# Linear attention and channel mix on one core: batch-wise groups in natural token order, v stationary in the K sums, list-scheduled issue, zero matmuls in early gaps

## The chip, the cores and the metric

The kernel runs on one core of one Trainium2 chip. The metric is the device time of one execution in microseconds (us). Each run has a state: it is called slow when it lies over 1.5% above the fastest of the same kernel. Engines: PE is TensorE (PEld its weight loads), DVE VectorE, ACT ScalarE, POOL GpSimd.

The runs were made on several chips.

## The reference

Four batches, four heads, 1088 tokens, head dimension 32, sketch rank 8; then a channel mix with width 128 and 1024 hidden channels.

```python
phi(x)  = outer(S1 x, S2 x)                      # 64 features per token and head
kv, z   = sum_s phi(k) v^T,  sum_s phi(k)        # over the 1088 tokens of a batch
x       = phi(q) kv / (phi(q) z + 1e-6)          # heads side by side: 128 channels
xk, xr  = mixes of x[s] and x[s-1] by mu_k, mu_r
out     = sigmoid(xr w_r) * (relu(xk w_k)^2 w_v)
```

No output of a batch can be formed before the K sums of that batch are complete; nothing ties one batch to another.

## The kernel before

It works on halves of two batches. A tile is 64 tokens of each, token `s*17+t`; half of k and q is transposed by DVE in 32x32 blocks, the other half by matmuls with the identity. The K sums have the features stationary:

```python
    def k_acc(half, gi, ab, kp):
        ...
        for t in range(t0, t1):
            for h in range(H):
                for b2 in range(2):
                    ...
                    nc.tensor.matmul(kv[hp:hp + 64, b2, (h // 2) * D:(h // 2) * D + D],
                                     kp[rows, t - t0, h].rearrange("p i j -> p (i j)"),
                                     tok["v%d" % half][rows, h, t, :], ...)
```

The order of issue is written by hand: first nearly all K work, with the q work of the first groups mixed in, then the channel mix of nine groups of up to 512 tokens, in which the q work of group g+3 is put between the matmuls of group g:

```python
    for n in range(nn + 3):
        g, cp = divmod(n, 4)
        if n < nn:
            mm1(g, cp)          # up-projection, then ReLU on ACT
        if cp == 0 and g + 3 < NQ:
            q1(g + 3)
        if cp == 1 and g + 2 < NQ:
            q5(g + 2)           # x = phi(q) kv, then PP on ACT and XK on DVE
        ...
        if n < nn:
            sq(g, cp)           # square on DVE
        if 2 <= n < nn + 2:
            mm2(*divmod(n - 2, 4))
```

`XK` is the mixed input of the up-projection: once it is written for a group, the group's eight matmuls, eight 512-column ReLUs and four squares can run.

## Time and profile before

The first three runs took 142.41, 143.49 and 229.2 us; the profiled execution has a span of 136.2 us.

| kernel before | us | share |
|---|---|---|
| PE busy | 98.8 | 73% |
| DVE busy | 78.3 | 57% |
| ACT busy | 69.2 | 51% |

No engine is full on average. Part 2 of the page, 40 equal slices of 3.4 us with the busy share in tenths, shows why: DVE and ACT have almost nothing to do from the fifth to the tenth slice and much to do in the second half.

```profile
PE   3250958659997789496929949549949689698970
DVE  3685030300158572285799595595396795977761
ACT  4010011101461423626886777674687767989950
```

The tile view of `wk`, the weights of the up-projection, says when the channel mix begins (durations in ns, then the first and last start in us):

```profile
L347 PE MATMUL h<-XK,wk x61: 270/379/634, 64.1 to 130.8; 128*128 128x512 bf16 x53, 128*128 128x256 bf16 x8
```

The first stands at 64.1 us, almost half way. The stretches of the view by windows give what each engine did from 12 to 36, from 36 to 60 and from 60 us on (after the length of the stretch the busy us of PE, PEld, DVE, ACT and POOL, each with its number of instructions in brackets; then the granted clock, the DMA share and GB/s):

```profile
12.00:36.00 24.00, 17.79 (x530) 15.89 (x534) 3.13 (x5) 2.90 (x7) 1.98 (x14) 0.93 0.76 181
36.00:60.00 24.00, 19.64 (x744) 16.88 (x736) 12.68 (x22) 9.82 (x25) 0.00 (x0) 1.00 0.02 4
60.00:136.00 76.00, 57.58 (x723) 39.53 (x730) 54.79 (x105) 54.27 (x82) 0.00 (x0) 0.97 0.08 31
```

In the first of them PE works 17.8 of 24 us and DVE 3.1. Much of PE's time before 60 us, 16.0 us in the first of these stretches and 10.7 in the second, is the K sums, lines L188 and L195: in all 9.6 + 6.5 + 11.3 = 27.4 us in the groups by form (busy us, mean ns; then the idle time before them):

```profile
L195 PE MATMUL kv<-ab 64*64 64x32 f32 x136 | 11.3, 243 | 0.0
L188 PE MATMUL kv<-tok_v_66,kp 64*64 64x32 f32 x272 | 9.6, 269 | 8.1 <-issue 4.5 <-DMA tok_v_66<-in_v_dram 3.6
L188 PE MATMUL kv<-tok_v_67,kp 64*64 64x32 f32 x272 | 6.5, 222 | 0.8 <-issue 0.8
```

### The profile page before, as it was taken

What the parts mean: (1) busy time and instruction counts of PE and PEld (TensorE: products, weight loads), DVE (VectorE), ACT (ScalarE), POOL (GpSimd) and SP (SyncE); (2) the same over time, 40 slices, a digit from 0 to 9 for tenths busy, and PEclk for the clock granted to TensorE, in tenths of its full rate; (3) what the DMA queues carried; (4) which work ended last, traced back from release to release, by engine and by line L of the source; (5) the groups of instructions that cost most, each with busy time, mean ns of one, the idle gap of its engine ahead of it and who ended that gap; (6) DMA issues with size and microseconds to landing.
All of it is one profiled execution on the core that took longest, in us unless ns stands there. A gap on an engine that the chain in (4) does not pass through costs nothing.

```text
span 136.2 us, 4574 instructions
## 1 busy us (share of the span) xinstructions
PE 98.8 (73%) x2054; PEld 75.1 (55%) x2065; DVE 78.3 (57%) x155; ACT 69.2 (51%) x117; POOL 8.4 (6%) x29
## 2 busy tenths in 40 slices
PE   3250958659997789496929949549949689698970
PEld 2140948458896658374626646346645466465650
DVE  3685030300158572285799595595396795977761
ACT  4010011101461423626886777674687767989950
POOL 7802004000000000000000000000000000000000
PEclk9999999986999999999999999986999999999998
DMA  3999999930000000000000002002002011021013
GB/s 103 335 275 305 301 248 224 302 58 5 5 5 0 5 5 5 7 0 5 0 2 5 0 0 82 0 0 77 0 0 82 0 40 42 0 77 76 5 77 115
DMA packets 5010, 9.79 MB, mean 72 GB/s; under 512 B 1520, under 2 KB 1904, under 8 KB 4992
## 3 DMA queue, kind: packets, MB, share of 16 engines
q1 hardware_dynamic: 3120, 6.69, 16.0%
q0 software_dynamic: 1856, 2.82, 8.9%
q8 instruction: 16, 0.26, 0.8%
q14 instruction: 2, 0.02, 0.0%
q10 hardware_dynamic: 16, 0.00, 0.0%
HBM read 7.80 MB, written 2.23 MB: 74 GB/s over the span
## 4 chain that ended last, share of the span: by engine, by line
PE 50%; DVE 18%; ACT 13%; DMA 8%; issue 8%; SPq 1%; DVEq 0%; ACTq 0%
PE kv L188 9%; DMA tok_v_66<-in_v_dram 8%; PE tp L154 8%; PE qtp L277 7%; PE o L367 7%; PE h L347 6%; DVE qp L270 5%; DVE XK L333 4%; PE abwp L250 4%; PE abp L166 4%; PE kv L195 3%; PE xps L317 2%; ACT PP_150 L332 2%; ACT PP_149 L332 2%; DVE den L262 1%
## 5 line engine op out<-in xcount | busy, mean ns | idle before, releaser
L174 DVE TENSOR_TENSOR kp<-ab 128x1024 f32<-128x1024 f32 (+1 forms) x10 | 10.6, 1064 | 23.3 <-ACT ab L170 23.1
L277 PE MATMUL qtp<-ident,qp 128*128 128x128 f32 x68 | 9.7, 284 | 13.9 <-DVE qp L270 11.8
L347 PE MATMUL h<-XK,wk 128*128 128x512 bf16 (+1 forms) x61 | 18.7, 374 | 0.5
L170 ACT COPY ab<-abp 128x256 f32<-128x256 f32 (+1 forms) x10 | 3.4, 341 | 26.6 <-PE abp L166 26.4
L277 PEld LDWEIGHTS qtp<-ident,qp 128*128 128x128 f32 x68 | 7.4, 142 | 16.9 <-ACT r L381 13.1
L188 PE MATMUL kv<-tok_v_66,kp 64*64 64x32 f32 x272 | 9.6, 269 | 8.1 <-issue 4.5
L188 PEld LDWEIGHTS kv<-tok_v_66,kp 64*64 64x64 f32 x272 | 8.9, 185 | 9.7 <-issue 9.7
L195 PE MATMUL kv<-ab 64*64 64x32 f32 x136 | 11.3, 243 | 0.0
L270 DVE TENSOR_TENSOR qp<-an,abw 128x1024 f32<-128x1024 f32 (+1 forms) x9 | 10.5, 1165 | 0.3
L317 PE MATMUL xps<-qpT,kvbd 128*64 128x256 f32 (+3 forms) x80 | 9.4, 359 | 0.0
L195 PEld LDWEIGHTS kv<-ab 64*64 64x64 f32 x136 | 8.6, 163 | 0.0
L283 ACT COPY qpT<-qtp 128x512 f32<-128x512 f32 (+1 forms) x9 | 5.1, 566 | 4.8 <-PE qtp L277 4.8
L166 PE MATMUL abp<-SW,kT_131 128*32 128x64 f32 x136 | 5.0, 314 | 3.5 <-DVE kT_131 L147 3.5
L285 DVE COPY qpT<-qtp 128x512 f32<-128x512 f32 (+1 forms) x9 | 5.9, 651 | 2.5 <-PE qtp L277 2.5
L188 PE MATMUL kv<-tok_v_67,kp 64*64 64x32 f32 x272 | 6.5, 222 | 0.8 <-issue 0.8
L333 DVE SCALAR_TENSOR_TENSOR XK<-xps,mu_k,PP_150 128x512 bf16<-128x512 f32 (+1 forms) x5 | 3.2, 644 | 6.5 <-ACT PP_150 L332 6.5
L188 PEld LDWEIGHTS kv<-tok_v_67,kp 64*64 64x64 f32 x272 | 5.9, 133 | 1.8 <-issue 1.5
L317 PEld LDWEIGHTS xps<-qpT,kvbd 128*64 128x64 f32 x80 | 4.5, 136 | 4.1 <-issue 1.7
L154 PE MATMUL tp<-ident,tok_k_68 128*32 128x128 f32 x136 | 6.5, 345 | 0.2 <-ACT qpT L283 0.2
L156 ACT COPY kT_132<-tp 128x512 f32<-128x512 f32 (+1 forms) x5 | 2.6, 523 | 7.9 <-PE tp L154 7.9
L347 PEld LDWEIGHTS <-wk 128*128 128x128 bf16 x72 | 5.7, 99 | 0.9 <-issue 0.7
L386 DVE TENSOR_TENSOR osb<-o,r 128x512 f32<-128x512 f32 (+1 forms) x9 | 5.9, 655 | 0.5 <-PE o L367 0.5
(235 smaller groups left out, 215.4 us busy)
## 6 DMA issues: line engine op xcount, KB each, us to landing
out_dram<-osb SPq DMA_DIRECT2D x7, 256.0 KB, 2.0
hd_k_70<-in_k_dram SPq DMA_DIRECT2D x1, 544.0 KB, 4.0
tok_v_66<-in_v_dram POOLq DMA_DIRECT2D x1, 544.0 KB, 8.4
hd_k_71<-in_k_dram SPq DMA_DIRECT2D x1, 544.0 KB, 5.7
tok_v_66<-in_v_dram SPq DMA_DIRECT2D x1, 544.0 KB, 11.5
tok_k_68<-in_k_dram POOLq DMA_DIRECT2D x1, 544.0 KB, 10.4
tok_k_68<-in_k_dram SPq DMA_DIRECT2D x1, 544.0 KB, 15.9
tok_q_69<-in_q_dram POOLq DMA_DIRECT2D x1, 544.0 KB, 12.5
```

Of the source, the lines that this page charges most:

```text
L154: nc.tensor.matmul(tp[D * h:D * h + D, t * P:t * P + P], tok[x][:, h, t0 + t, :], ident[:], skip_group_check=True, tile_position=(0, D * h))
L166: nc.tensor.matmul(abp[32 * c:32 * c + 32, t * 64:t * 64 + 64], kT[half][:, t0 + t, 32 * c:32 * c + 32], SW[:, 0, :, :2, :], skip_group_ch ...
L174: nc.vector.tensor_mul(kp[:, :n], _ap(a_, list(a_.ap[1:]) + [[0, R]]), _ap(b_, list(b_.ap[1:3]) + [[0, R]] + [b_.ap[3]]))
L188: nc.tensor.matmul(kv[hp:hp + 64, b2, (h // 2) * D:(h // 2) * D + D], kp[rows, t - t0, h].rearrange("p i j -> p (i j)"), tok["v%d" % half] ...
L195: nc.tensor.matmul(kv[:64, b2, 64:64 + HR], ab[rows, t - t0].rearrange("p h x r -> p (h x r)"), ab[rows, t - t0, :, 1, :], start=False, st ...
L270: nc.vector.tensor_mul(qp[g][:, :n], _ap(a_, list(a_.ap[1:]) + [[0, R]]), _ap(b_, list(b_.ap[1:3]) + [[0, R]] + [b_.ap[3]]))
L277: nc.tensor.transpose(p[:, t * P:t * P + P], qp[g][:, t, 2 * pair:2 * pair + 2].rearrange("p h i j -> p (h i j)"), ident[:])
L285: nc.vector.tensor_copy(o, p[:, :n * P])
L317: nc.tensor.matmul(o[64 * pair:64 * pair + 64], kvbd[:, 2 * half + b2, pair, :], qpT[g][:].rearrange("p r t (b s) -> p r t b s", b=2)[:, p ...
L333: nc.vector.scalar_tensor_tensor(XK[:, half * NT + T:half * NT + T + m, :].rearrange("p t s -> p (t s)"), src, mu_k[:], PP[half][:, T:T + ...
L347: nc.tensor.matmul(h[:, c, :n * P], wk[:, (2 * cp + c) * P:(2 * cp + c + 1) * P], XK[:, 4 * g:4 * g + n, :].rearrange("p t s -> p (t s)"))
L367: nc.tensor.matmul(ops[g][:, t * P:t * P + P], k2[:, c, t * P:t * P + P], wv[:, 2 * cp + c, :], start=(cp == 0 and c == 0 and t == 0), sto ...
```

## The change

The change rewrites the kernel. Its intent: let the channel mix of the first batch start while the later batches are still being summed. Tokens stay in natural order, ten groups of 256 or 512 tokens run through the batches, all k and q are transposed by DVE, and the K sums have v stationary (32 columns to load) with the 64 features moving. The order of issue comes from a small scheduler: every piece of work is a task with an engine, an assumed duration, dependencies, a PSUM bank to open and a due time counted back from the output of its group; a task may not start more than 7 us before it is due, and otherwise each engine takes what can start first. Up to a planned time of 17 us, PE's planned gaps are filled with matmuls on zeros, so as to keep its clock up. The core of the diff:

```diff
+class Plan:
+    LAT = {"PE": 0.16, "ACT": 0.20, "DVE": 0.14, "DMA": 0.0}
...
+    def run(self, window):
...
+        for t in reversed(order):
+            d = 1e9 if t["due"] is None else t["due"]
+            for s in succ[t["name"]]:
+                d = min(d, s["d"] - s["us"] - self.LAT[s["eng"]])
+            t["d"] = d
...
+        clock = {e: 0.0 for e in self.LAT}
...
+                    r = max(r, t["d"] - window - t["us"])
+                    key = (max(r, clock[e] + 0.02), t["d"], t["i"])
...
-                    nc.tensor.matmul(kv[hp:hp + 64, b2, (h // 2) * D:(h // 2) * D + D],
-                                     kp[rows, t - t0, h].rearrange("p i j -> p (i j)"),
-                                     tok["v%d" % half][rows, h, t, :],
+                nc.tensor.matmul(kv[32 * h:32 * h + 32, :64], vt[b][:, h, T, :],
+                                 kp[:, t, h].rearrange("p i j -> p (i j)"),
...
+    def q_trans(b, hf):
+        o = qT[:, b * S:(b + 1) * S].rearrange("p (a t) -> p t a", t=2 * U)
+        nc.vector.transpose(o[:, U * hf:U * hf + U], hdq[b][:, U * hf:U * hf + U, :])
...
+    T0, PER = 14.0, 1.95
...
+        add(f"FN{g}", "DVE", dve(N), lambda g=g: fin(g), [f"M2{g}_3", f"SG{g}"], uses=[f"o_{g}"], due=T0 + PER * (G0[g] + n) + 4)
...
+    seq = plan.run(7.0)
+    wt = psum.tile([P, 512], F32, name="wt", tag="o0")
+    WARM = 17.0
+    pe = 1.6
+    for t in seq:
+        if t["eng"] == "PE":
+            if t["start"] < WARM:
+                for _ in range(max(0, int((t["start"] - pe - 0.1) / 0.23))):
+                    nc.tensor.matmul(wt[:], zero[:, :P], zero[:], skip_group_check=True)
+            pe = t["start"] + t["us"]
+        if t["fn"]:
+            t["fn"]()
```

## The prediction

> **What bounds it now.** The span is 136.2 us; the runs took 142.4 and 143.5 us (a third, 229 us, I ignore). No engine is full (page: PE 73%, DVE 57%, ACT 51%), but its two halves are run one after the other. The tile view of `wk` puts the first up-projection matmul at 64.1 us. Before that it forms K sums and projections: by stretches, DVE works 3.1 of the 24 us from 12 to 36, ACT 2.9, PE 17.8; the chain is the wait for v (to 13.6 us), then K sums, matmul transposes and projections on PE. After 64 us nine groups take about 7.8 us each, with DVE 58 to 83% busy; the chain hops between engines, with dependence bubbles (DVE `XK` on ACT `PP` 11.3 us in total, PE `qtp` on DVE `qp` 11.8).
>
> **What the change does.**
> - K sums: lines L188 and L195 hold 27.4 us of PE busy, 680 pairs of load and matmul. With v stationary, 45 per batch: 180. From the timeline, four warm 128-token tiles cost 1.5 us before; I estimate 0.8 after.
> - Transposes of k1 and q0 leave PE (11.1 us busy) and ACT (about 5 us) and go to DVE, about +6 us there (0.38 us a start for 256 columns).
> - Batch by batch with 2- and 4-tile groups: the FFN should start near 16 to 18 us (k0, v0, q0 and then weights at the measured 250 to 330 GB/s) instead of 64. This is the large term.
> - Most `qpT` evictions leave DVE for ACT; ReLUs become single-bank (0.48 us a start).
>
> **Budgets after** (start-to-start intervals from the timelines at 96 to 108 us), per group of 512: DVE small ops 1.27, `qp` 1.2, `XK` 0.67, four squares 2.44, output 0.6: 6.2 us; 8.5 groups 52.5. K and the transposes, 5.8 per batch, 23. DVE about 77 us. PE: up 1.73, down 1.8, gate 0.45, transposes 0.9, x 1.0, projection 0.8: 6.7, times 8.5 = 57, plus K about 17: 74. ACT about 61. DVE and PE, nearly level, become the limit: from about 5.5 us (first k on chip), at 87 to 92% use, work ends at 89 to 94; the last groups' drain and output add about 3.
>
> **The zero matmuls.** The Trainium skill ("TensorE: Matmul & The Clock Gate", the HAM clock gate) says that PE runs at half clock until about 3.4 us of sustained work. The trace agrees: the first four tiles of K sums took 2.77 us, the third four 1.49. The fill is sized from a planned time of 1.6 us, but setup matmuls end near 4.3 us (trace) and precede it in order; about 18 of 512 columns (estimate 0.43 us cold, 0.22 warm) would run to about 9 or 10 us and delay the first projection by 2 to 3 us. They buy back about as much: neutral within 2 us.
>
> **Prediction.** Span about 95 us, time 102 us, 0.71 of before; range 94 to 112. Chances: faster 0.97, same 0.02, slower 0.01.
>
> **What would show it.** First up-projection before 22 us; DVE over 80% busy from 10 to 85 us; K sums under 14 us of PE; the chain mostly DVE with PE; DVE waiting on ACT or PE much below before.
>
> **What would make it wrong.** Weights, queued behind the first k and sharing the engines with the loads, landing after 20 us. The planned order not matching the chip: in-order engines and three auxiliary banks then make new waits and DVE stays under 75%: 110 us or more.  If overlap is nearly perfect: 93.

## The result, and the profile after

The time fell to 112.88 us in the median of four runs (112.87, 112.72 and 112.88 fast, 114.67 slow), with 142.95 us in the median for the kernel before (four runs, that of 229.2 us among them): 0.811 of before, 95% interval 0.803 to 0.819. Ratios are the mean time of one kernel's fast runs over that of the other's of the same rounds, so not quite the ratio of the medians. (The ratio of the medians is 0.790.) The forecast of "clearly faster" held; the figure did not. 102 us had been said, with 112 at the top of the range.

The span of the profiled run is 111.1 us. Busy shares in slices of 2.8 us:

```profile
PE   0689976996999997899999975999768499898960
DVE  6280296699999999899999994678996347967860
ACT  5000200345869733899696357999536799898950
```

PE is busy 91.5 us (82%), DVE 84.7 us (76%), ACT 67.2 us (61%). By the tile view of `wk` the first up-projection moved from 64.1 to 27.2 us:

```profile
L530 PE MATMUL ps_h<-XK,wk x80: 269/379/390, 27.2 to 105.9; 128*128 128x512 bf16 x56, 128*128 128x256 bf16 x24
```

By the groups by form the K sums cost PE 7.2 + 3.8 = 11.0 us instead of 27.4:

```profile
L378 PE MATMUL ps_kv<-kp,vt 128*32 128x64 f32 x288 | 7.2, 224 | 2.5 <-DVE kp L333 2.3
L384 PE MATMUL ps_kv<-ab 128*32 128x32 f32 x72 | 3.8, 194 | 0.0
```

So far the mechanism is the one predicted. Two stretches are not. The first is the start. These are lines of the timeline, three of PE and two of DVE (start us, duration us, what, count, in square brackets the idle time before and who ended it):

```profile
3.75 0.76 PE L314 MATMUL sps<-S,selx 8*128 8x128 f32 x2 [3.75 <-DMA S<-in_S_dram]
6.29 5.90 PE L626 MATMUL wt<-zero 128*128 128x512 bf16 x19
12.12 1.27 PE L350 MATMUL ps_kab<-SW,kT 128*64 128x64 f32 x36
...
7.12 1.48 DVE L343 STREAM_TRANSPOSE kT<-hdk 128x256 f32<-128x256 f32 x4
13.26 2.85 DVE L333 TENSOR_TENSOR kp<-ab 128x512 f32<-128x512 f32 x4 [4.65 <-ACT ab L357]
```

The transposed k of batch 0 is there at 7.12 + 1.48 = 8.60 us, the first part earlier, but the projection that reads it starts at 12.12 us, behind 19 zero matmuls that run from 6.29 us on. DVE stands idle for 4.65 us. The Trainium skill ("TensorE: Matmul & The Clock Gate", Step-by-step: what each phase is for) says that matmuls stay in program order; the trace agrees: the projections begin as the last zero matmul ends, at 12.12 us.

The second is the end. Four stretches of 6 us (busy us of PE, PEld, DVE, ACT, POOL):

```profile
60.00:66.00 6.00, 5.74 (x114) 4.45 (x111) 5.90 (x13) 1.83 (x5) 0.00 (x0) 1.00 0.16 46
66.00:72.00 6.00, 4.00 (x34) 2.12 (x32) 3.50 (x7) 5.20 (x13) 0.00 (x0) 1.00 0.00 0
78.00:84.00 6.00, 4.24 (x54) 3.21 (x52) 5.79 (x15) 2.62 (x8) 0.00 (x0) 1.00 0.23 72
84.00:90.00 6.00, 4.42 (x34) 2.24 (x32) 2.68 (x7) 4.71 (x12) 0.00 (x0) 1.00 0.03 8
```

In these two pairs DVE and ACT take turns: where DVE works 5.8 or 5.9 of 6 us, ACT works 1.8 or 2.6, and in the stretch after it the reverse. (Between the pairs, from 72 to 78 us, both are busy, 5.0 and 6.0 us.) The writes of `XK` on DVE show what the turns are. Each of these lines hands one group of 512 tokens to the channel mix, in one operation or, where two batches meet in the group, in two (the view prints the size of one). The seventh such group follows at 93.8 us; three groups of 256 stand at the ends, one before and two after:

```profile
31.71 0.67 DVE L517 SCALAR_TENSOR_TENSOR XK<-ps_x,mu_k,PP 128x512 bf16<-128x512 f32 x1
45.71 0.88 DVE L517 SCALAR_TENSOR_TENSOR XK<-ps_x,mu_k,PP 128x320 bf16<-128x320 f32 x2 [0.34 <-ACT XB L523]
53.01 0.74 DVE L517 SCALAR_TENSOR_TENSOR XK<-ps_x,mu_k,PP 128x512 bf16<-128x512 f32 x1
67.18 0.81 DVE L517 SCALAR_TENSOR_TENSOR XK<-ps_x,mu_k,PP 128x384 bf16<-128x384 f32 x2
71.18 0.75 DVE L517 SCALAR_TENSOR_TENSOR XK<-ps_x,mu_k,PP 128x512 bf16<-128x512 f32 x1 [0.86 <-ACT PP L512]
86.68 0.88 DVE L517 SCALAR_TENSOR_TENSOR XK<-ps_x,mu_k,PP 128x448 bf16<-128x448 f32 x2 [1.50 <-ACT XB L523]
```

Groups arrive unevenly: at 31.7, then 45.7 and 53.0, then 67.2 and 71.2, then 86.7 us. Three times 14 to 15.5 us pass without a new one, and the engines that live on `XK` run dry. Three lines of the timeline of PE, ACT and DVE from that time:

```profile
68.03 0.81 PE L530 MATMUL ps_h<-XK,wk 128*128 128x512 bf16 x3 [2.00 <-DVE XK L517]
62.70 1.07 ACT L498 COPY qpT<-ps_qtp 128x512 f32<-128x512 f32 x2 [2.71 <-PE ps_qtp L489]
69.63 0.69 DVE L542 TENSOR_TENSOR k<-k 128x1024 bf16<-128x1024 bf16 x1 [1.64 <-ACT k L536]
```

From 10 to 85 us DVE is nearly full all the same, 64.9 of 75 us (the view by windows):

```profile
10.00:85.00 75.00, 66.31 (x1041) 44.98 (x1039) 64.90 (x138) 45.93 (x112) 3.46 (x4) 1.00 0.34 86
```

The span can be split by DVE, which is on the chain most (43% of it by the page). The predicted span of about 95 us was made of 5.5 until k is on the chip, 77 of work, 12.5 of idle time with the output's end. Measured: 7.1 us until the first transpose; 84.7 - 3.3 (busy before that) = 81.4 of work; and 111.1 - 7.1 - 81.4 = 22.6 of idle time with the end. The 16.1 us too little are thus 1.6 of start, 4.4 of work and 10.1 of idle time. Of the 22.6 us, 4.65 are the wait at the fill.

### The profile page after: what moved, and what is told of

Read it like the earlier page. It is cut to its first block, busy times and chain, and to the rows that moved or that the text cites. A ratio compares the mean times of both kernels' runs of the same rounds, so it can differ in the third digit from the quotient of the medians.

```text
span 111.1 us, 3029 instructions
## 1 busy us (share of the span) xinstructions
PE 91.5 (82%) x1243; PEld 59.8 (54%) x1243; DVE 84.7 (76%) x192; ACT 67.2 (61%) x166; POOL 9.1 (8%) x27
## 4 chain that ended last, share of the span: by engine, by line
DVE 43%; PE 28%; ACT 18%; issue 5%; DMA 2%; DVEq 0%; ACTq 0%
ACT k L536 11%; DVE k L542 7%; DVE kp L333 7%; DVE qT L441 6%; PE wt L626 6%; DVE qp L333 5%; PE ps_h L530 4%; PE ps_x L506 4%; PE ps_o L552 3%; DVE osb L577 3%; DVE XK L517 3%; ACT PP L512 3%; DVE kT L343 3%; PE ps_kab L350 3%; DMA S<-in_S_dram 2%
## 5 line engine op out<-in xcount | busy, mean ns | idle before, releaser
L536 ACT ACTIVATE k<-ps_h 128x512 bf16<-128x512 f32 (+1 forms) x80 | 36.7, 558 | 3.4 <-PE ps_h L530 3.2
L542 DVE TENSOR_TENSOR k<-k 128x1024 bf16<-128x1024 bf16 (+1 forms) x40 | 23.6, 604 | 7.3 <-ACT k L536 6.6
L530 PE MATMUL ps_h<-XK,wk 128*128 128x512 bf16 (+1 forms) x80 | 21.9, 348 | 4.6 <-DVE XK L517 4.3
L552 PE MATMUL ps_o<-wv,k 128*128 128x128 bf16 x272 | 21.6, 220 | 1.6 <-DVE k L542 1.4
L552 PEld LDWEIGHTS <-k 128*128 128x128 bf16 x272 | 16.4, 98 | 7.6 <-DVE k L542 4.7
L333 DVE TENSOR_TENSOR kp<-ab 128x512 f32<-128x512 f32 (+1 forms) x16 | 11.7, 756 | 4.7 <-ACT ab L357 4.7
L489 PE MATMUL ps_qtp<-ident,qp 128*128 128x128 f32 x68 | 10.9, 283 | 1.9 <-DVE qp L333 1.2
L498 ACT COPY qpT<-ps_qtp 128x512 f32<-128x512 f32 (+1 forms) x18 | 9.2, 549 | 5.1 <-PE ps_qtp L489 5.1
L333 DVE TENSOR_TENSOR qp<-an,ps_abw 128x512 f32<-128x512 f32 (+1 forms) x20 | 11.2, 599 | 0.1
L506 PE MATMUL ps_x<-qpT,kvbd 128*64 128x512 f32 (+7 forms) x52 | 9.5, 462 | 0.0
L441 DVE STREAM_TRANSPOSE qT<-hdq 128x544 f32<-128x544 f32 x8 | 9.0, 1189 | 0.0
```

What stands on the lines that cost most here:

```text
L333: nc.vector.tensor_mul(o.rearrange("p t h i j -> p (t h) i j"), _ap(a_, [[sa, y], [1, R], [0, R]]), _ap(b_, [[sb, y], [0, R], [1, R]]))
L441: nc.vector.transpose(o[:, U * hf:U * hf + U], hdq[b][:, U * hf:U * hf + U, :])
L489: nc.tensor.transpose(p[:, t * P:t * P + P], qp[g][:, t, 2 * pair:2 * pair + 2].rearrange("p h i j -> p (h i j)"), ident[:])
L506: nc.tensor.matmul(p[64 * pair:64 * pair + 64, c0:c0 + m], kvbd[:, b, pair, :], qpT[g][:, pair, c0:c0 + m], skip_group_check=True, tile_po ...
L530: nc.tensor.matmul(h[:, :n * P], wk[:, c * P:(c + 1) * P], XK[:, G0[g] * P:(G0[g] + n) * P])
L536: nc.scalar.activation(k1s[g, c // 2][:, c % 2, :n * P], tiles[f"h_{g}_{c}"][:, :n * P], RELU)
```

## The experiments

The theory after reading the trace: the idle time is made by the order of issue. The plan hands DVE whatever can start first, the k work of later batches among it, so groups reach the channel mix late and in pairs, and ACT, which has done only 33.0 of its 67.2 us by 66 us, cannot catch up. Rivals: ACT's capacity alone sets the end; the zero matmuls at the start; slow q transposes. All kernels but `e2_qline` and `e3_both` gave correct results.

### Zero matmuls and the stride of the q transposes

`e1_nofill` takes the zero matmuls away:

```diff
-    WARM = 17.0
+    WARM = 0.0
```

> The changed kernel without its zero matmuls. Fill theory: the 19 zero matmuls after the setup hold the first k projection from 8.0 to 12.1 us and DVE idles 4.65 us for it, so the time falls by 3 to 4.5 us (112.9 to about 109) although PE is cold for the first microseconds. Rival (the fill buys back what it costs, as predicted): within 1.5 us of 112.9, with K sums of batch 0 taking nearly twice as long.

`e2_qline` lets each q transpose write consecutive columns instead of every 34th:

```diff
-        o = qT[:, b * S:(b + 1) * S].rearrange("p (a t) -> p t a", t=2 * U)
+        o = qT[:, b * S:(b + 1) * S].rearrange("p (t a) -> p t a", t=2 * U)
```

> The eight q transposes write each block in consecutive columns instead of every 34th (wrong result on purpose). Stride theory: one of them falls from about 1.1 us to 0.6 us, DVE busy by about 4 us, the time by 2 to 4 us. Rival (the transpose costs 1.1 us whatever the stride): no change.

`e3_both` has both edits.

> Both of the above. If both costs lie on the chain: the sum of the two gains, about 5 to 8 us (105 to 108). If one is absorbed by later idle time: little more than the larger one.

| run (one chip) | fast runs, us | ratio to before |
|---|---|---|
| e1_nofill | 109.8, 109.75 | 0.775 |
| e2_qline | 111.5 to 112.4 | 0.790 |
| e3_both | 107.6 to 108.6 | 0.762 |

The record calls the class of the ratios of this call (`e1_nofill` to `e4_order`) unclear (intervals up to 0.024 to either side); they stand for some 141.7 us of before, where its two fast runs took 139.71 and 140.69. So the times themselves are compared.

Without the fill DVE waits 0.90 us instead of 4.65, and the projections run slower. The projections on PE and the features on DVE again, from the timeline of `e1_nofill`:

```profile
7.63 2.42 PE L350 MATMUL ps_kab<-SW,kT 128*64 128x64 f32 x36 [1.35 <-DVE kT L343]
...
9.43 2.77 DVE L333 TENSOR_TENSOR kp<-ab 128x512 f32<-128x512 f32 x4 [0.90 <-ACT ab L357]
```

The 36 projections take 2.42 us instead of 1.27, nearly double, which agrees with the half clock of a cold PE in the Trainium skill (the page and section named in the prediction). It is read from the durations alone: the clock column of the view by windows shows 1.00 over the 2.42 us (7.6 to 10.1 us). Still the features start at 9.43 instead of 13.26 us. In time, the fill costs 4 us between `e2_qline` and `e3_both`, both in one call (fast runs 112.0 and 108.0 us in the mean); between the change and `e1_nofill`, in two calls, the difference is 3 us by the times (112.8 and 109.8) and 5 by the ratios. The prediction's "neutral within 2 us" was wrong: the projections behind the fill gained 1 us by the shorter durations, after 4.5 us of delay (12.12 against 7.63 us).

The stride matters too. The transposes of q in the groups of instructions of the change (busy us, mean ns):

```profile
L441 DVE STREAM_TRANSPOSE qT<-hdq 128x544 f32<-128x544 f32 x8 | 9.0, 1189 | 0.0
```

and in those of `e2_qline`:

```profile
L441 DVE STREAM_TRANSPOSE qT<-hdq 128x544 f32<-128x544 f32 x8 | 5.6, 725 | 0.0
```

The same instruction on the same sizes takes 1189 ns when it writes every 34th column and 725 ns in a row. In time this is worth 1.8 us without the fill (`e1_nofill` 109.8, `e3_both` 108.0 us). What it is worth with the fill in place is not shown: `e2_qline` has 112.0 us where the change has 112.8. It was run at another time. The Trainium skill ("VectorE: DVE Perf Modes", The three transpose paths) gives one figure for a DVE transpose, 311 ns for 128x128 bf16, and in this section nothing on the stride of its output.

### The order of issue

`e4_order` has no fill and issues the same instructions in another order. The plan gets durations, release delays and engine start times as the trace has them, due times closer together, no hold-back window, and ReLU and squares rank 6 us later, so that the way of the next group to `XK` goes first. Which of a kind's PSUM banks a tile takes is also the plan's choice and changes with it; the number of banks does not.

```diff
-    LAT = {"PE": 0.16, "ACT": 0.20, "DVE": 0.14, "DMA": 0.0}
+    LAT = {"PE": 0.20, "ACT": 0.20, "DVE": 0.15, "DMA": 0.0}
...
+        for t in order:
+            t["d"] += 6.0 if t["name"][:2] in ("RE", "SQ") else 0.0
...
-        clock = {e: 0.0 for e in self.LAT}
+        clock = {"PE": 6.4, "ACT": 0.0, "DVE": 7.1, "DMA": 0.0}
...
-            add(f"QT{b}_{hf}", "DVE", 0.08 + 0.00104 * 32 * U, ...
+            add(f"QT{b}_{hf}", "DVE", 1.06, ...
-        add(f"QN{g}", "DVE", 2 * dve(32 * n) + dve(36 * n) + dve(32 * n) + 0.05, ...
+        add(f"QN{g}", "DVE", (1.20 if n == 4 else 0.98), ...
-    T0, PER = 14.0, 1.95
+    T0, PER = 14.0, 1.42
-    seq = plan.run(7.0)
+    seq = plan.run(100.0)
```

> No zero matmuls, and the same instructions issued in another order: the plan gets measured durations and engine start times, due dates closer together, no hold-back window, and lower priority for ReLU and squares, so the next group's chain to XK runs ahead. Order theory (DVE idles 12 us after 66 us because the next group's chain stands behind squares in program order): 9 to 11 us below the run without fill, about 98 to 101 us. Capacity theory (after 66 us ScalarE is 87% busy and is the limit): at most 3 us below the run without fill.

(The 87% in it are not in the trace: from 66 to 111 us of the change ACT is busy 34.2 of 45 us, 76%.)

Measured: 99.55 us in the median (99.35 to 100.77), 0.705 of before, where `e1_nofill` on the same chip has 109.8 us and 0.775. Ten us less with the same instructions: DVE is busy 84.0 us here and 84.9 there, ACT 67.1 and 67.2, PE, whose ends are modelled, 82.2 and 86.8. The mean granted clock was 0.999 here and 0.968 there; in the repeat of both on another chip (below) it was 0.994 and 1.000, with the same gain, so the clock is not the cause. The capacity theory, at most 3 us, falls. The groups now reach the channel mix 8 to 10 us apart:

```profile
27.90 0.75 DVE L519 SCALAR_TENSOR_TENSOR XK<-ps_x,mu_k,PP 128x512 bf16<-128x512 f32 x1 [0.43 <-ACT XB L525]
36.67 0.87 DVE L519 SCALAR_TENSOR_TENSOR XK<-ps_x,mu_k,PP 128x320 bf16<-128x320 f32 x2
46.03 0.75 DVE L519 SCALAR_TENSOR_TENSOR XK<-ps_x,mu_k,PP 128x512 bf16<-128x512 f32 x1 [0.21 <-ACT XB L525]
55.77 0.88 DVE L519 SCALAR_TENSOR_TENSOR XK<-ps_x,mu_k,PP 128x384 bf16<-128x384 f32 x2 [0.25 <-ACT XB L525]
64.55 0.75 DVE L519 SCALAR_TENSOR_TENSOR XK<-ps_x,mu_k,PP 128x512 bf16<-128x512 f32 x1
72.86 0.88 DVE L519 SCALAR_TENSOR_TENSOR XK<-ps_x,mu_k,PP 128x448 bf16<-128x448 f32 x2 [0.47 <-ACT XB L525]
```

and ACT has done 41.0 us of its work by 66 us instead of 33.0, with DVE fuller up to that mark (60.2 of 66 us against 54.5). The two stretches in the view by windows of the change (PE, PEld, DVE, ACT, POOL):

```profile
0.00:66.00 66.00, 56.85 (x891) 37.78 (x892) 54.51 (x128) 33.01 (x82) 9.06 (x27) 1.00 0.48 126
66.00:111.00 45.00, 34.62 (x353) 22.05 (x351) 30.23 (x65) 34.23 (x85) 0.00 (x0) 1.00 0.10 31
```

and in that of `e4_order`:

```profile
0.00:66.00 66.00, 55.12 (x930) 40.84 (x934) 60.16 (x139) 41.03 (x101) 7.58 (x27) 1.00 0.47 125
66.00:97.50 31.50, 27.10 (x285) 18.10 (x283) 23.84 (x54) 26.04 (x65) 0.00 (x0) 1.00 0.15 47
```

This corrects the capacity theory rather than only denying it: from 66 us on the change has 34.2 us of ACT work left, so no run of it could end before 100. But that debt was made earlier, by the order.

`e5_calib` takes only the true inputs of the plan, `e6_prio` only the altered rule of choice; both without fill.

> No fill, and only the plan's inputs made true (start of PE 6.4 and DVE 7.1 us, a q transpose 1.06 us, the four small operations 1.2 us, release delays 0.20 and 0.15 us); the rule of choice unchanged. If wrong inputs spoiled the order: most of the 11 us that the reordered kernel gained over the one without fill, so 100 to 103. If the rule of choice did: within 3 us of the run without fill (108 to 110.6).

> No fill, inputs of the plan as in the change, and only the rule of choice altered (due dates closer, no hold-back, ReLU and squares 6 us later in rank). If the rule spoiled the order: 100 to 104. If it needs both: each alone 2 to 4 us below the run without fill, 106 to 109.

Measured: 108.47 us (0.780 of before) and 106.19 us (0.766), on a second chip. The run without fill was repeated on a third, as `e9_nofill2`, beside `e4_order`'s repeat:

> The run without fill once more, as the reference for the other three on this chip: the kernel before came out at 143.2 us in one call and 138.8 in the other, so runs of the two calls can't be set side by side. Expected 108 to 111 us.

> The reordered kernel again, as the reference for the next: 9 to 11.5 us below the run without fill, 98 to 101 us.

They took 110.3 us (0.797) and 100.67 us (0.728): both edits together gain 9.5 us on one chip. For each edit alone the reference ran on another chip. By the bare ratios, true inputs alone gain 0.016 of before (2.3 us, with 139 us for before), the rule alone 0.031 (4.3 us). But one kernel, the one with features stationary (`e8_kstat`, `e10_kstat2`, below), ran in both calls, and its ratio was 0.012 lower in the call of `e5_calib` and `e6_prio`. It gives a better estimate: it lay 2.9 us above the run without fill on the one chip, so that run would take about 112.3 - 2.9 = 109.4 us on the other (fast runs in the mean), and true inputs alone gain about 1 us (108.4, within the noise), the rule alone about 3 (106.4). Either way the sum is less than the 9.5 us of both. Of the outcomes written down, "needs both" holds for `e6_prio`; `e5_calib` fits "the rule of choice did" as well. Which of the three parts of the rule (due times, window, rank) does most was not separated. Nor is even spacing of the groups enough: in `e6_prio` the `XK` of the first six groups of 512 stand at 30.5, 41.5, 51.5, 61.7, 71.2 and 80.7 us, evenly, but 10 us apart where `e4_order` has 9, and DVE has done 57.4 us of work by 66 us instead of 60.2. That the order makes the idle time is shown; that it does so by the pairs of groups is read from the traces.

### The overlap of batches

`e7_allk` makes every q projection wait for the K sums of all batches; otherwise it is the run without fill.

```diff
-            ... + [f"KW{b}" for b in bs],
+            ... + [f"KW{b}" for b in bs] + ["KW3"],
```

> No fill, and every q projection made to wait until the K sums of all four batches are done, so the batch-wise overlap is undone. Overlap theory (it is the large term of the gain): the first up-projection moves from 23 to some 45 us and the time rises by about 12 us over the run without fill, to about 122. Rival (the gain is the smaller amount of PE work): less than 4 us more.

Measured: 126.25 us, 0.905 of before, against 0.797 for the run without fill on another chip: 15 us more by the ratios, 16 against the estimate of 109.4 us above, somewhat over the 12 expected. The channel mix begins at 45.2 us:

```profile
L530 PE MATMUL ps_h<-XK,wk x80: 269/378/390, 45.2 to 117.8; 128*128 128x512 bf16 x56, 128*128 128x256 bf16 x24
```

So the overlap is the largest single part of the gain: the whole gain of the change without fill is 0.203 of before, 28 us, and 15 to 16 of them go when the batches are no longer overlapped. Two things go with the edit and were not separated: the plan, and so the order of issue, is made anew, and the granted clock was 0.66 to 0.69 from 15 to 45 us here, against 1.00 in `e9_nofill2`. The Trainium skill ("Perfetto Trace Analysis", Optimization Strategy) says that interleaving regimes in which different engines are the most contended may help; this pair of runs agrees, with 15 to 16 us.

### v stationary

`e8_kstat` puts the features back as the stationary operand. The sum then has the layout that the next step wants, so four small transposes and a copy per batch fall away.

```diff
-                nc.tensor.matmul(kv[32 * h:32 * h + 32, :64], vt[b][:, h, T, :],
-                                 kp[:, t, h].rearrange("p i j -> p (i j)"), ...
+                nc.tensor.matmul(kv[hp:hp + 64, (h // 2) * D:(h // 2) * D + D], kp[:, t, h].rearrange("p i j -> p (i j)"),
+                                 vt[b][:, h, T, :], ...
```

> No fill, and the features stationary in the K sums again with v moving (64 columns loaded, 32 moved; the sum then has the layout of the kernel before, and four small transposes per batch and one copy fall away). If PE's time in K sums matters: 2 us or more slower. If PE is off the chain there, since DVE is full from 24 to 66 us: within 1.5 us of the run without fill, either way.

It took 112.09 us, but without its reference on that chip; so it was run again as `e10_kstat2` beside `e9_nofill2`.

> The features stationary in the K sums again, beside its reference on the same chip. If v stationary is worth time: 2 to 4 us above the run without fill, of which about 2.2 us arise before the first q projection, where batch 0 is alone and PE is cold. If the earlier 112.1 came from the chip: within 1 us of the reference.

Measured: 113.09 us (0.818) against 110.3 us (0.797), 2.8 us more. The first K sums of batch 0 on the timeline of PE, with v stationary (`e9_nofill2`):

```profile
10.23 0.65 PE L378 MATMUL ps_kv<-kp,vt 128*32 128x64 f32 x16
```

and with the features stationary (`e10_kstat2`):

```profile
10.18 1.07 PE L379 MATMUL ps_kv<-vt,kp 128*64 128x32 f32 x16
```

Sixteen take 0.65 us one way and 1.07 us the other. The last K sums of batch 0 start at 12.79 us in the one and at 15.37 us in the other, and the first q projection at 16.02 and 17.43 us. But this lead is gone by the first write of `XK`, 24.39 against 24.44 us, and the first up-projection stands at 25.0 us in both. The delay that lasts arises later: the second group's `XK` stands at 29.51 and 31.89 us, the one after the long gap at 84.47 and 86.70, and the spans are 108.9 and 111.1. The expectation that 2.2 us arise before the first q projection does not hold. And since the edit alters tasks of the plan, the order of issue changes with it; whether the 2.8 us come from the K sums' time on PE (17.7 instead of 12.5 us busy) or from the order was not separated.

### A version that beats both

`e12_best` starts from `e4_order`, loads S1 first, puts six zero matmuls where PE waits during setup, ranks the kinds of work more finely, and gives the ReLU results ten buffers.

```diff
+    RANK = {"RE": 6, "SQ": 10, "M1": 2, "XK": -2, "KW": -4, "XB": 2, "QT": 4, "QE": 2}
...
+    nc.sync.dma_start(S8[:, 0, :], S1)
     load_k(0, nc.sync)
-    nc.scalar.dma_start(S8[:, 0, :], S1)
...
-            k1s[g, c // 2] = work.tile([P, 2, 512], BF16, name="k1", tag="k1", bufs=4)
+            k1s[g, c // 2] = work.tile([P, 2, 512], BF16, name="k1", tag="k1", bufs=10)
```

(Three other pools lose one or two buffers to make room; the engine start times and the due times of the plan follow.)

> The reordered kernel with S1 loaded first on the other queue (setup ends near 5.3 instead of 7.1 us), six zero matmuls that stand only where PE waits during setup, a finer ranking of the kinds of work, and more buffers for the ReLU results. DVE is the limit: the earlier start should give 1.5 to 2 us and the ranking 1 to 2, so 95 to 97.5 us. If the fill warms PE in time, the 36 projections take under 2 us instead of 2.4.

Measured: 99.38 us (98.78 to 99.73), 0.719 of before, against 100.67 us (0.728) for `e11_order2` on the same chip: 1.3 us better, less than expected. DVE's first transpose of k started at 6.52 us, where `e4_order` has 7.07 us, not at 5.3: the setup matmuls start at 3.09 us, only 0.66 us before those of the change (3.75), and what they wait for is no longer S but DVE's `selx`. The few zero matmuls did what they are for: the projections took 1.83 us, not 2.42. Which of the edits made the 1.3 us was not separated. It is the best version, 99.4 us where the change has 112.9 (by the ratios 0.719 and 0.811). It was run at another time.

## Why the prediction was right or wrong

- **Direction and mechanism: right.** The early start of the channel mix ("FFN" in the prediction) was called "the large term", and `e7_allk` shows 15 to 16 us for it. The start itself was said at 16 to 18 us and was 27.2. The weights did not hold it (`wk`, issued at 5.5 us, landed 7.2 us later), but batch 0's own chain: 3 us of it are the fill (24.1 us in `e1_nofill`), and why the rest is longer than estimated was not followed up. An early start is not enough, the channel mix has to be fed in time after it: in `e4_order` the first up-projection in the trace stands at 24.0 us, hardly sooner than the 24.1 of `e1_nofill`, and the time is 10 us less.
- **K sums: right.** Under 14 us of PE was said, 11.0 measured. In time they are worth 2.8 us (`e10_kstat2`), with the change of order that goes with the edit.
- **"DVE and PE, nearly level, become the limit: at 87 to 92% use": this is the step that failed.** DVE did reach that use from 10 to 85 us (64.9 of 75 us, 87%), so the sign named in the prediction appeared; but over the whole of its work, from 7.1 us to the end, it was 81.4 of 104.0 us, 78%. Idle time with the end was 22.6 us instead of 12.5. `e9_nofill2`, without the fill, still has 108.9 - 7.1 - (84.8 - 3.3) = 20.3 us; `e11_order2`, same instructions, same chip, other order, has 99.2 - 7.1 - (84.1 - 3.3) = 11.3 us. So 9.0 us of the idle time were made by the order of issue, in which groups reached the channel mix in pairs and DVE ran short after each pair. The budgets were nearly right, and the step from level budgets to a full engine was not: the prediction took the planned order for a good one. It named the alternative itself ("the planned order not matching the chip ... 110 us or more"), and that came, with DVE at 76%, just above the 75% it named.
- **DVE's work, about 77 us: too low by 4.4.** The largest term that was mis-sized is the q transposes, costed from 0.38 us for 256 columns. At that rate 544 columns would take 0.81 us (an estimate); at the stride of 34 they take 1189 ns, 3.0 us more over eight, and 725 ns without it (`e2_qline`). The rest of the 4.4 was not traced.
- **The zero matmuls, "neutral within 2 us": wrong.** They cost about 4 us. Both terms were off: the setup matmuls ended near 6.3 us, not 4.3, because S landed late (the first waits for its DMA until 3.75 us), so the fill ran to 12.1 us instead of 9 or 10 and delayed the first projection by 4.5 us instead of 2 to 3; and what it bought back was about 1 us.
- **Time over span: wrong in the other direction.** 7 us were added to the span, from the profile of before (136.2) and timed runs of before. Those were different executions. In one and the same run the difference is 1.8 us (112.87 and 111.1; for before 139.71 and 137.9). So the span was missed by 16 us and the time by 11: by luck the second error hid 5 us of the first.

## What to carry to other kernels

Level busy sums say where a pipeline could end, not that it gets there: look at when the operation that releases the bottleneck's work (here the write of `XK`) happens, and how long the gaps between such writes are. If a scheduler in the source makes the order, give it measured durations, delays and start times, and let the work that feeds the next group go before the work that finishes this one: here only both together gave most of the gain. Put fill for the clock only where the engine waits by measurement, not by plan, since here the projections behind it in program order waited too, and it cost about 4 us.

## What the Trainium skill lacked or had wrong

- "VectorE: DVE Perf Modes", The three transpose paths: in this section no word on the stride of the output (what the skill says elsewhere of strided access to SBUF gives no figure for a DVE transpose). A 128x544 f32 transpose took 1189 ns when it wrote every 34th column and 725 ns when it wrote them in a row; with every second column, four transposes of 256 columns of k took 1.48 us, 370 ns each.
- "Perfetto Trace Analysis", Optimization Strategy: says that the same gap repeating can mean too few buffers, which is not wrong, but the section does not name the order of issue as a cause. Here, with the same number of PSUM banks and buffers, another order took DVE's idle time with the end from 20.3 (`e9_nofill2`) to 11.3 us (`e11_order2`).
- "TensorE: Matmul & The Clock Gate", the HAM clock gate: right here (2.42 against 1.27 us for the same 36 projections), but it does not say that filling can cost more than it gains: 19 zero matmuls gained about 1 us in the projections and cost about 4 us in time.
